# ScalarE's order in a fused layer: the second norm's deviations of tiles 2 and 3 ahead of two passes over tile 0

## The chip, the cores and the metric

The kernel runs on one core of a Trainium2 chip. The time is device microseconds of one execution. A core has five engines with an instruction queue each, worked off in order: TensorE (PE, with its weight loads PEld), VectorE (DVE), ScalarE (ACT), GpSimd (POOL) and SyncE (SP), which here only issues DMAs. An instruction that waits for a semaphore holds up everything behind it on its own engine.

## What is computed

One layer over a sequence of 2048 rows of 512 numbers, in bfloat16. A vector c, through SiLU and w_mod, gives six modulation rows. Then two branches, each with a residual:

```python
h = _layernorm(x) * (1 + ca) + sa
x = x + ga * A(h)          # dilated local attention, 32 heads of 16, window 8, dilation 2
h = _layernorm(x) * (1 + cb) + sb
x = x + gb * B(h)          # B norms h once more, then an MLP over the rows (2048 -> 1792 -> 2048)
```

So every row is normed three times: before the attention (norm 1), after it (norm 2, then scaled and shifted), and at the start of the MLP (norm 3). The MLP mixes rows, so it needs all tiles of rows for each of its 14 blocks of hidden units; the kernel adds up the products of the tiles as they become ready.

## The kernel before

The rows are 16 tiles of 128. The attention runs over five chunks of 2, 4, 4, 4 and 2 tiles (0 to 4); tiles 2 to 5 are chunk 1. Several chunks are under way at once. The kernel's helper functions do not emit instructions: they register named steps with their dependencies, and a text, ORDER, names all steps in the order in which they are emitted. An engine thus gets its steps in the order in which they stand in ORDER. A letter behind a colon picks the engine where a step has a choice (a is ScalarE, d VectorE, p POOL, s SyncE; q is a form of the matmul with four groups of columns). PSUM banks and the large work buffers are given out along ORDER too: a step that needs one takes the free one that was freed first in ORDER.

Steps that the change and the prediction speak of:

- `x1_t`, `ln2q_t`: ScalarE copies the residual sum of tile t out of PSUM, with its row sum, and then squares the deviations, with their sum. Both sums lie in `sums`.
- `rstd2_g`: the inverse deviations of norm 2 for a group of tiles that starts at g, two ScalarE instructions, `lv` = Ln(scaled sum + eps) and `rs` = Exp(-lv/2). Groups of chunk 1 are tiles 2, 3 and tiles 4, 5. `nb2_g` on VectorE makes the offset from the mean and `rs`; `n2_t` applies both; `aff_g` scales and shifts a group (two pairs of VectorE operations in all for tiles 2 to 5).
- `ln3s_t`, `ln3v_t`, `rstd3_g`, `nb3_g`, `h3_t`: the same for norm 3, statistics, their last step on VectorE, inverse deviations, offsets, normed tile. For tiles 0 and 1 the statistics are two ScalarE passes (a mean, then squares of what is left) into `mv`. For tiles 3 and 5 they are two ScalarE passes too, with a small VectorE operation (`ln3v3`, `ln3v5`) behind them; for 2 and 4 VectorE's batch statistics and an aggregate (`ln3v2`, `ln3v4`). `h3_0` and `h3_1` run on POOL, `h3_2` and `h3_3` on VectorE, `h3_4` and `h3_5` on ScalarE.
- `ev4_tj`: ScalarE copies queries (t = 0), keys (1) or values (2) of chunk 4 out of PSUM.
- `qk`, `red`, `max`, `sub`, `exp`, `esum`, `rcp`, `smB`, `a2`, `pv`, `pvacc`, `oev`, `wo`: the attention of a chunk. VectorE multiplies queries and keys (`qk`), TensorE sums (`red`), VectorE takes the maximum (`max`), TensorE subtracts it (`sub`), ScalarE takes the exponent (`exp`), TensorE sums it (`esum`), ScalarE inverts the sum (`rcp`, its result `rb`), VectorE scales (`smB`, in `lsb`), DMAs of SyncE rearrange (`a2`), VectorE multiplies with the values (`pv`), TensorE sums (`pvacc`), ScalarE copies out (`oev`), TensorE projects (`wo`).
- `mlp1_...`: the MLP's first matmuls, over a few tiles `h3` at a time.

The code behind `rstd`:

```python
nc.scalar.activation(lv[:, sl, 0], mv[:, sl, 1] if var is None else var, ACT.Ln, scale=vscale, bias=epscol[:, 0:1])
nc.scalar.activation(rs[:, sl, 0], lv[:, sl, 0], ACT.Exp, scale=-0.5)
```

In ORDER, ScalarE has around the place `ln2q2`, `ev4_20`, `ln3s0`, `ev4_12`, `rstd2_2`, `ev4_22`, `oev2_0`, `rstd2_4`, `n2_2`, `exp3`, `oev2_3`, `n2_5`, `rcp3`, `n2_4`, `oev2_2`, `rstd3_0`, `oev2_1`, `ev4_02`, `ln3s3`, `ev4_00`, `rstd3_2`. VectorE has `qk3_3`, `pv2_0`, `nb2_2`, `max3`, `pv2_2`, `nb2_4`, `pv2_1`, `smB3`, `aff2`, `aff4`, `nb3_0`, `ln3s2`, `ln3v3`, `ln3v2`, `ln3s4`, `ln3v4`, `h3_3`, `h3_2`, `pv3_1`. All instructions carry the line of the wrapper that emits them, L143, so the profile's rows are told apart by their operands and their time.

Of the kernel before, what the change touches and what calls it, by code (L numbers as in the profile page):

```python
# [213 lines left out]
fill:1:q vd2_0 oev1_0:a oev1_1:a pvacc1_3 ev3_11:a qk3_1 qkv3_23:q oev1_3:a a2_2_2:s ln3s1 qkv3_03:q wo4:q a2_2_1:s  # L214
qk3_2 a2_2_0:s ev3_03:a ev3_23:a x1_4:a ln2q4 wo2:q x1_2:a a2_2_3:s red3_0 wo3:q x1_3:a ln2q3 qkv3_21:q ev3_21:a wo5:q
red3_1 pv2_3 x1_5:a vd2_2 qk3_3 qkv4_20:q red3_2 qkv4_22:q red3_3 qkv4_12:q fill:18:q ln2q5 ld_w1_0_512 ln2q2 pv2_0
pvacc2_0 vd3_0 ev4_20:a ln3s0 ev4_12:a rstd2_2 ev4_22:a qkv4_02:q oev2_0:a rstd2_4 nb2_2 n2_2:a max3 sub3:q exp3
pvacc2_3 oev2_3:a qkv4_10:q pv2_2 vd3_2 esum3:q nb2_4 pv2_1 vd3_1 n2_3:p ld_w1_0_0 n2_5:a rcp3 smB3 pvacc2_2 fill:14:q
a2_3_0:s a2_3_1:s a2_3_3:s n2_4:a qkv4_00:q oev2_2:a rstd3_0 aff2 pvacc2_1 oev2_1:a wo6:q wo9:q wo7:q aff4 nb3_0
ln3s2:d ev4_02:a ln3s3:a ln3v3 h3_1:p wo8:q a2_3_2:s ev4_00:a ln3v2 ld_w2_0 ln3s4:d rstd3_2 x1_9:a ln3s5:a h3_0:p  # L220
# [857 lines left out]
```

## Time and profile before

| | us |
|---|---|
| three runs | 199.3, 199.72, 200.41 (median 199.72) |
| the profiled execution | 199.64 |
| its span, first to last instruction | 197.9 |
| mean granted TensorE clock | 0.999 |
| PE, DVE, ACT, POOL busy | 187.8, 157.5, 127.8, 18.5 |

The span is 1.74 us shorter than the execution's own time. A row of the timeline gives start, length, engine, operation, output and inputs, shapes and a count, and in brackets the time that the engine stood idle before it, with what ended the wait. Starts are from the first instruction. Instructions on one engine overlap a little: the next one starts some hundredths of a microsecond before the one ahead has written its last result.

### The profile page before, as it was taken

What the parts mean: (1) busy time and instruction counts of PE and PEld (TensorE: products, weight loads), DVE (VectorE), ACT (ScalarE), POOL (GpSimd) and SP (SyncE); (2) the same over time, 40 slices, a digit from 0 to 9 for tenths busy, and PEclk for the clock granted to TensorE, in tenths of its full rate; (3) what the DMA queues carried; (4) which work ended last, traced back from release to release, by engine and by line L of the source; (5) the groups of instructions that cost most, each with busy time, mean ns of one, the idle gap of its engine ahead of it and who ended that gap; (6) DMA issues with size and microseconds to landing.
All of it is one profiled execution on the core that took longest, in us unless ns stands there. A gap on an engine that the chain in (4) does not pass through costs nothing.

```text
span 197.9 us, 5606 instructions
## 1 busy us (share of the span) xinstructions
PE 187.8 (95%) x2348; PEld 101.9 (51%) x2358; DVE 157.5 (80%) x222; ACT 127.8 (65%) x305; POOL 18.5 (9%) x45
## 2 busy tenths in 40 slices
PE   2999999999999988999999999999999999999993
PEld 0586655655456676544544454444444444444453
DVE  2789999999999998999999999986564254726554
ACT  3898997998999999999999799833760000000000
POOL 4164002000100001030001100500000000000000
PEclk9999999999999999999999999999999999999999
DMA  5999985728678756379299367588999201111611
GB/s 171 325 358 321 219 227 164 156 57 260 230 223 285 236 191 215 105 159 298 40 332 227 76 209 143 156 241 233 329 224 325 74 0 53 39 44 53 172 53 53
DMA packets 53893, 36.02 MB, mean 182 GB/s; under 512 B 24428, under 2 KB 50668, under 8 KB 53868
## 3 DMA queue, kind: packets, MB, share of 16 engines
q1 hardware_dynamic: 52228, 35.21, 63.0%
q10 hardware_dynamic: 1640, 0.46, 1.0%
q8 instruction: 18, 0.29, 0.6%
q14 instruction: 7, 0.06, 0.1%
HBM read 22.55 MB, written 2.10 MB: 125 GB/s over the span
## 4 chain that ended last, share of the span: by engine, by line
PE 64%; ACT 19%; DVE 5%; DMA 4%; SPq 3%; issue 3%; ACTq 0%; DVEq 0%
PE psS L143 63%; ACT junk L143 4%; DMA vD<-v_sb 3%; SPq L143 3%; ACT xx L143 2%; ACT v_sb L143 2%; ACT h L143 2%; DVE big L143 2%; PE psL L143 2%; ACT q_sb L143 2%; ACT k_f L143 2%; DVE h L143 1%; ACT o_sb L143 1%; DMA c_t<-in_c_dram 1%; ACT lsb L143 1%
## 5 line engine op out<-in xcount | busy, mean ns | idle before, releaser
L143 PEld LDWEIGHTS <-wst 128*128 128x128 bf16 (+1 forms) x584 | 35.6, 101 | 33.0 <-issue 2.8
L143 PE MATMUL psS<-h,wst 128*32 128x512 bf16 (+1 forms) x358 | 50.5, 379 | 0.6 <-issue 0.2
L143 DVE TENSOR_TENSOR big<-q_sb,k_f 128x4096 bf16<-128x4096 bf16 (+1 forms) x20 | 36.6, 1857 | 0.1
L143 DVE TENSOR_TENSOR big<-a2sb,vD 128x4096 bf16<-128x4096 bf16 (+1 forms) x20 | 36.5, 1858 | 0.0
L143 PE MATMUL psS<-hT,w_qkv 128*32 128x512 bf16 (+1 forms) x576 | 29.6, 344 | 0.3 <-ACT o_sb L143 0.3
L143 DVE SCALAR_TENSOR_TENSOR h<-psS,bcol,rows_bc 128x512 f32<-128x512 f32 (+2 forms) x17 | 12.1, 710 | 22.1 <-PE psS L143 20.6
L143 PEld LDWEIGHTS <-w_qkv 128*32 128x32 bf16 (+1 forms) x618 | 22.1, 107 | 14.1 <-issue 0.5
L143 PE MATMUL psS<-gT,big 128*128 128x512 bf16 x110 | 24.7, 379 | 0.1
L143 PEld LDWEIGHTS <-big 128*128 128x128 bf16 x144 | 12.1, 98 | 13.8 <-DMA big<-in_w_mod_dram 0.5
L143 PE MATMUL psS<-woq,o_sb 128*32 128x512 bf16 (+1 forms) x207 | 16.7, 379 | 0.5 <-ACT o_sb L143 0.5
L143 ACT ACTIVATE gT<-psS,bcol 128x512 bf16<-128x512 f32 x14 | 9.0, 686 | 8.3 <-DVE psS L143 8.2
L143 POOL TENSOR_SCALAR h<-xx,rs,nb 128x512 bf16<-128x512 bf16 x9 | 7.0, 785 | 72.7 <-DVE nb L143 33.9
L143 DVE TENSOR_TENSOR psS<-psS,gT 128x512 f32<-128x512 f32 x14 | 9.3, 695 | 5.0 <-PE psS L143 5.0
L143 PE MATMUL psS<-hT,wst 128*32 128x512 bf16 (+2 forms) x135 | 11.7, 355 | 0.1
L143 ACT ACTIVATE h<-xx,nb,rs 128x512 bf16<-128x512 bf16 x15 | 11.6, 812 | 0.0
L143 DVE TENSOR_TENSOR h<-h,xx 128x512 bf16<-128x512 f32 (+2 forms) x17 | 11.1, 653 | 0.6
L143 PEld LDWEIGHTS <-group 128*32 128x32 bf16 x288 | 7.8, 96 | 7.2 <-issue 2.7
L143 DVE BATCH_NORM_STATS2 st<-xx 128x6 f32<-128x512 bf16 x12 | 8.0, 682 | 4.3 <-DMA xx<-in_A_x_dram 4.2
L143 DVE TENSOR_TENSOR h<-h,rows_bc 128x1024 bf16<-128x1024 bf16 (+2 forms) x16 | 10.9, 689 | 0.4
L143 ACT ACTIVATE junk<-xx,sums 128x512 bf16<-128x512 bf16 x14 | 10.1, 722 | 1.6 <-DVE xx L143 1.4
L143 ACT ACTIVATE v_sb<-psS,qvb 128x512 bf16<-128x512 f32 (+1 forms) x20 | 11.0, 597 | 0.0
L143 PEld LDWEIGHTS <-ident 128*32 128x32 bf16 (+2 forms) x242 | 7.1, 99 | 7.4 <-issue 2.8
(107 smaller groups left out, 252.4 us busy)
## 6 DMA issues: line engine op xcount, KB each, us to landing
vD<-v_sb SPq DMA_DIRECT2D x12, 524.5 KB, 3.7
big<-in_B_w_dram SPq DMA_DIRECT2D x4, 896.0 KB
vD<-v_sb SPq DMA_DIRECT2D x8, 268.5 KB, 5.1
wst<-in_B_w_dram SPq DMA_DIRECT2D x3, 640.0 KB
out_dram<-h SPq DMA_DIRECT2D x15, 128.0 KB, 1.8
wst<-in_B_w_dram SPq DMA_DIRECT2D x2, 800.0 KB
xx<-in_A_x_dram SPq DMA_DIRECT2D x6, 256.0 KB, 8.0
gT<-in_w_mod_dram SPq DMA_DIRECT2D x4, 384.0 KB, 4.7
```

The costliest lines, as they stand in the source:

```text
L143: r = fn(*a, **k)
```

## The change

One name in ORDER moves. `rstd2_2` stood behind `ev4_12` and now stands behind `ev4_20`, so ScalarE emits its two instructions ahead of `ln3s0` (the third norm's two passes over tile 0) and `ev4_12`. Its inputs are the sums that `ln2q2` and `ln2q3` leave. All other steps keep their order on every engine, and the step takes and frees no buffer.

```diff
-pvacc2_0 vd3_0 ev4_20:a ln3s0 ev4_12:a rstd2_2 ev4_22:a qkv4_02:q oev2_0:a rstd2_4 nb2_2 n2_2:a max3 sub3:q exp3
+pvacc2_0 vd3_0 ev4_20:a rstd2_2 ln3s0 ev4_12:a ev4_22:a qkv4_02:q oev2_0:a rstd2_4 nb2_2 n2_2:a max3 sub3:q exp3
```

## The prediction

> **What bounds the kernel now.** I read the engine totals and the chain of waits first, then a table of stretches around the edited place, then the waits and the timelines there. The page:
>
> ```profile
> PE 187.8 (95%) x2348; PEld 101.9 (51%) x2358; DVE 157.5 (80%) x222; ACT 127.8 (65%) x305; POOL 18.5 (9%) x45
> ...
> PE 64%; ACT 19%; DVE 5%; DMA 4%; SPq 3%; issue 3%; ACTq 0%; DVEq 0%
> ```
>
> TensorE sets most of the span, but 19% of the chain is ScalarE. Where that lies, the stretches show (length; busy time of PE, weight loads, DVE, ACT, POOL; granted clock; DMA):
>
> ```profile
> 72.00:76.00 4.00, 3.33 (x99) 2.44 (x95) 3.12 (x4) 3.94 (x12) 0.00 (x0) 1.00 0.64 239
> 76.00:82.00 6.00, 5.39 (x172) 3.90 (x164) 6.00 (x5) 5.94 (x14) 0.77 (x1) 1.00 0.72 227
> 82.00:87.00 5.00, 4.51 (x88) 2.03 (x80) 4.90 (x13) 4.73 (x15) 1.71 (x3) 1.00 0.27 64
> 87.00:92.00 5.00, 4.88 (x92) 2.36 (x84) 5.00 (x7) 4.94 (x18) 0.00 (x0) 1.00 1.16 297
> ```
>
> From 72 to 92 us ScalarE is never free: 3.94 of 4 us, 5.94 of 6, 4.94 of 5. VectorE is equally full except in the first stretch, where 0.88 us are missing. The waits between 72 and 94 us name that hole and one more on ScalarE:
>
> ```profile
> DVE nb L143 <- ACT rs L143: 0.9, 1, 0.9
> ...
> ACT lv L143 <- DVE mv L143: 0.2, 1, 0.2
> ```
>
> These are the two joints of the forecast. The chain of waits shows where ScalarE hands the end over to TensorE (start, length, what):
>
> ```profile
> 92.30 1.42 ACT h L143 x2
> 93.72 0.04 issue
> 93.76 3.09 PE psS L143 x52
> ```
>
> So h3_4 and h3_5 (the two "ACT h") release matmuls at 93.76, and from there on the chain is TensorE's own work almost to the last instruction. A gain on ScalarE at 92 us reaches the end; a gain on VectorE alone does not.
>
> **The change part by part.** The step rstd2_2 is two ScalarE instructions (Ln into lv, Exp into rs), with no DMA, nothing on SP or POOL, no buffer taken or freed. ScalarE in the order of time:
>
> ```profile
> 72.63 0.82 ACT L143 ACTIVATE v_sb<-psS,qvb 128x256 bf16<-128x256 f32 x2
> ...
> 74.81 0.57 ACT L143 ACTIVATE k_f<-psS 128x512 bf16<-128x512 f32 x1
> 75.29 0.28 ACT L143 ACTIVATE lv<-sums,epscol 128x2 f32<-128x2 f32 x1
> 75.60 0.20 ACT L143 ACTIVATE rs<-lv 128x2 f32<-128x2 f32 x1
> 75.71 0.82 ACT L143 ACTIVATE v_sb<-psS,qvb 128x256 bf16<-128x256 f32 x2
> ...
> 80.45 0.31 ACT L143 ACTIVATE rb<-ls 128x128 bf16<-128x128 f32 x1
> ```
>
> *Moved earlier.* The pair occupies 75.71 - 75.29 = 0.42 us. It goes to where the first v_sb row ends, 72.63 + 0.82 - 0.09 = 73.36 (an instruction here starts about 0.09 before the one ahead has drained: 74.81 + 0.57 = 75.38 against 75.29). rs is then there at about 73.87 instead of 75.80. Nothing is added or removed, so ScalarE's work from 72.63 to 75.71 is the same length, and v_sb at 75.71 stays.
>
> *Moved later.* The third norm's two passes over tile 0 (ln3s0) and the key copy ev4_12 come 0.42 later. The first is needed by rstd3_0, behind the rb row above, five microseconds on. The copy frees a PSUM bank at 75.38, now 75.80; by the kernel's bank rule its next taker is the sum of exponents, and the keys themselves are read only by chunk 4's products, behind all of chunk 3's in VectorE's queue:
>
> ```profile
> 79.11 0.63 PE L143 MATMUL psS<-lsb,ident 128*32 128x128 bf16 x32
> ```
>
> That leaves 3.3 us of cover; both cost nothing. Without the cover the price would be the 0.42.
>
> *VectorE.* Its timeline, with idle time and releaser in brackets:
>
> ```profile
> 72.67 2.28 DVE L143 TENSOR_TENSOR big<-a2sb,vD 128x4096 bf16<-128x4096 bf16 x1
> 75.84 0.16 DVE L143 SCALAR_TENSOR_TENSOR nb<-sums,rs 128x2 f32<-128x2 f32 x1 [0.88 <-ACT rs L143]
> 75.92 1.22 DVE L143 TENSOR_REDUCE m<-psL 128x128 bf16<-128x1024 f32 x1
> 77.05 2.28 DVE L143 TENSOR_TENSOR big<-a2sb,vD 128x4096 bf16<-128x4096 bf16 x1
> ...
> 79.32 2.29 DVE L143 TENSOR_TENSOR big<-a2sb,vD 128x4096 bf16<-128x4096 bf16 x1
> 81.52 0.68 DVE L143 TENSOR_TENSOR lsb<-lsb,rb 128x1024 bf16<-128x1024 bf16 x1
> ...
> 83.45 1.41 DVE L143 TENSOR_TENSOR h<-h,rows_bc 128x1024 bf16<-128x1024 bf16 x2
> ...
> 84.78 0.15 DVE L143 SCALAR_TENSOR_TENSOR nb<-mv,rs 128x2 f32<-128x2 f32 x1
> 84.85 0.69 DVE L143 BATCH_NORM_STATS2 st<-h 128x6 f32<-128x512 bf16 x1
> 85.45 0.43 DVE L143 SCALAR_TENSOR_TENSOR mv<-mv,st 128x1 f32<-128x1 f32 x1
> 85.81 0.17 DVE L143 BATCH_NORM_AGGREGATE mv<-st 128x2 f32<-128x6 f32 x1
> ```
>
> nb2_2 (75.84) stood 0.88 us with everything behind it: max3, pv2_2, nb2_4, pv2_1, smB3. With rs there at 73.87 it starts at 74.96, or 74.88 with the usual overlap; the queue gains 0.88 to 0.96. What is late next is rb: smB3 needs it, and ScalarE ends it at 80.45 + 0.31 = 80.76, unmoved. pv2_1 would be through at 81.52 - 0.88 = 80.64 at the latest, so smB3 starts at 80.79 (0.03 after rb, as 75.84 followed 75.60 + 0.20 by 0.04). VectorE keeps 0.73 of 0.88. On TensorE, sub3 starts earlier, but its sum of exponents at 79.11 waits for exp3 on ScalarE, ahead of which no instruction waits for VectorE: TensorE's hole only moves.
>
> *What ScalarE gets back.* It is full, so only waits of its own can shrink. There are three, each read as start minus (end of the one before, minus 0.09):
>
> ```profile
> 82.16 0.20 ACT L143 ACTIVATE rs<-lv 128x2 f32<-128x2 f32 x1
> 82.33 0.60 ACT L143 ACTIVATE o_sb<-psS 128x512 bf16<-128x512 f32 x1
> 82.82 0.83 ACT L143 ACTIVATE q_sb<-psS,qvb 128x256 bf16<-128x256 f32 x2
> 83.63 0.63 ACT L143 ACTIVATE junk<-h 128x512 bf16<-128x512 bf16 x1
> ...
> 84.92 0.19 ACT L143 ACTIVATION_READ_ACCUMULATOR junk<-h 128x1 f32 x1
> 85.02 0.82 ACT L143 ACTIVATE q_sb<-psS,qvb 128x256 bf16<-128x256 f32 x2
> 86.01 0.29 ACT L143 ACTIVATE lv<-mv,epscol 128x2 f32<-128x2 f32 x1 [0.17 <-DVE mv L143]
> ```
>
> 1. o_sb at 82.33 (oev2_1) against 82.36 - 0.09 = 82.27: 0.06. It waits for matmuls fed by pv2_1. TensorE may keep part of it, so 0 to 0.06; I take 0.04.
> 2. junk at 83.63 (ln3s3) against 83.65 - 0.09 = 83.56: 0.07. It waits for aff2, done as the second pair of "h" operations starts at 83.45; with VectorE 0.73 ahead it waits no more.
> 3. lv at 86.01 (rstd3_2) against 85.84 - 0.09 = 85.75: 0.26, if its mv is ready in time.
>
> Is it? ln3v3 (the 0.43 us row at 85.45) needs ln3s3's read, 84.92 + 0.19 = 85.11, less 0.11 from items 1 and 2: 85.00, so it starts at 85.03, VectorE being there since 85.45 - 0.73 = 84.72. At most 0.43 us long, it and the 0.17 us aggregate end by 85.03 + (85.81 - 85.45) + 0.17 = 85.56, plus 0.03: 85.59. ScalarE reaches its lv at 85.75 - 0.11 = 85.64. Just in time, so item 3 counts whole.
>
> The sum is 0.04 + 0.07 + 0.26 = **0.37 us** (bounds: 0 if item 3 and the others are taken away by the rivals below, 0.88 if the whole hole came through). ScalarE has no other wait up to 93.72, so h3_5 ends 0.37 earlier. TensorE stands waiting there:
>
> ```profile
> 93.76 1.20 PEld L143 LDWEIGHTS <-wst 128*32 128x32 bf16 x27 [0.45 <-issue]
> ```
>
> 0.45 is more than 0.37, so TensorE can take all of it; the stalls before it follow ScalarE's copies too and shrink alike. Past 94 us loads are issued when TensorE releases their buffers, so they move along.
>
> One resource can spoil item 3. POOL forms h3_1 and h3_0 right after VectorE's nb3_0, beside ln3v3:
>
> ```profile
> 85.11 1.53 POOL L143 TENSOR_SCALAR h<-h,rs,nb 128x512 bf16<-128x512 bf16 x2 [8.18 <-DVE nb L143]
> ...
> 89.51 0.21 DVE L143 SCALAR_TENSOR_TENSOR mv<-mv,st 128x1 f32<-128x1 f32 x1
> ```
>
> The same operation takes 0.21 with POOL idle and 0.43 beside POOL, ending at 85.88, when half of POOL's 1.53 is over (85.11 + 0.77). The Trainium skill, "SBUF — State Buffer", section "SBUF: two separate sides", says that VectorE with two SBUF inputs and GpSimd take a shared port pair as an exclusive lock, the loser blocked for a whole instruction; by that rule the two rows agree, and an arrival behind the second POOL instruction would wait for that one's end. After the change POOL starts at 84.78 - 0.73 + (85.11 - 84.78) = 84.38 and passes from h3_1 to h3_0 at 85.15; ln3v3 arrives at 85.03, only 0.12 before. I take the near side, with the rival below as the far one.
>
> **The numbers.** The profiled execution took 199.64 us (span 197.9 and 1.74 around it); 199.64 - 0.37 = 199.27. That execution is 0.08 under the median of 199.72, so I put the figure for a median at 199.3.
>
> **The rivals.**
> - *The hole comes through whole*: 199.64 - 0.88 = 198.76. For it: VectorE is as full as ScalarE from 76 us on, and every later instruction of it was queued behind the hole. Against: rb at 80.76 and ln3s3 are ScalarE's, and no wait of ScalarE before 82.33 depends on VectorE. Chance 0.15.
> - *Nothing arrives*: the bracket at 93.76 reads "issue", not "ACT h". If another thing, such as a weight buffer, released TensorE there, its stream keeps its place: 199.64, or 199.60 with item 1. Against: h ends 93.72, 0.04 before. Chance 0.14.
> - *Slower, through POOL*: if ln3v3 is ready after 85.15, it is held until h3_0 ends, 84.38 + 1.53 = 85.91. Ending there, as the row of 85.45 ended with its POOL instruction, it puts lv at 85.91 - 0.07 + 0.17 + 0.03 = 86.04: 0.03 later than now, 199.67. Starting only there, it adds its 0.21: lv at 86.25, 0.24 later, 199.88. It decides from a slip of 0.12 us in my chain of starts on. For it: the slip is the size of three unknown overlaps. Against: those rows give the near side. Chance 0.14.
>
> **How the numbers follow.** The forecast has 0.47, the rivals 0.15, 0.14 and 0.14, and 0.10 is left for what I don't see, half on each side. The likeliest case alone spans 199.15 to 199.5. To hold 8 in 10, the range takes in the rivals and the scatter of the shown runs (199.3 to 200.41, which moves a median by some tenths): 198.6 to 200.0. A measurement of this kernel tells about 0.5%, 1 us, from no change. Faster by more than that (below 198.72): half of the first rival 0.08, a tenth of the forecast through scatter 0.05, half of the unseen 0.05: 0.18. Slower (above 200.72): a third of the POOL rival through scatter 0.05, 0.04 from the forecast and the second rival, 0.05 unseen: 0.14. Within: 0.68.
>
> **What would show it.** Right: the 0.88 bracket before nb2_2 gone; max3 near 74.95; a new short wait of VectorE for rb, smB3 near 80.8; lv of rstd3_2 near 85.64 without a bracket; the chain's passage from ACT h to PE near 93.4; a span near 197.5. The first rival would show smB3 at 80.64 or before, with rb earlier than 80.76. The POOL rival would show mv<-mv,st ending with the second POOL instruction near 85.9. The second would show TensorE still starting at 93.76 with h long done. I am wrong altogether if ScalarE's starts between 75.71 and 82 us shift by more than 0.1, or if the granted clock in these stretches leaves 1.00.

## The result, and the profile after

| | us | ratio to before (95% interval) |
|---|---|---|
| before, 22 runs beside it | median 199.55 (199.21 to 201.13) | |
| after, 22 runs | median 199.04 (198.82 to 200.0) | 0.9969 (0.9956 to 0.9982) |
| after, measured once more: 11 runs, before 199.67 | median 199.33 (199.01 to 199.65) | 0.9981 (0.9971 to 0.9992) |

The kernel is faster by 0.2 to 0.3%: the first ratio says 0.62 us (the two medians alone differ by 0.51), the second 0.38. The trace says 0.42 from the edited place to the end, which both intervals hold. The profiled execution took 199.34 us with a span of 197.6.

First the waits of the changed kernel between 72 and 94 us (who waited for whom, us in total, times, longest):

```profile
PE psS L143 <- ACT lsb L143: 0.8, 1, 0.8
...
DVE mv L143 <- ACT junk L143: 0.2, 1, 0.2
DVE lsb L143 <- ACT rb L143: 0.2, 1, 0.2
```

VectorE's 0.9 for rs is gone, and so is ScalarE's 0.2 for mv. In their place VectorE waits twice for ScalarE, 0.2 each. TensorE's hole of 0.6 ahead of sub3 is now one of 0.8 ahead of the sum of exponents. VectorE's timeline (start, length, operation, idle time before it):

```profile
72.80 2.29 DVE L143 TENSOR_TENSOR big<-a2sb,vD 128x4096 bf16<-128x4096 bf16 x1
75.00 0.15 DVE L143 SCALAR_TENSOR_TENSOR nb<-sums,rs 128x2 f32<-128x2 f32 x1
75.07 1.22 DVE L143 TENSOR_REDUCE m<-psL 128x128 bf16<-128x1024 f32 x1
...
80.91 0.69 DVE L143 TENSOR_TENSOR lsb<-lsb,rb 128x1024 bf16<-128x1024 bf16 x1 [0.15 <-ACT rb L143]
...
85.13 0.22 DVE L143 SCALAR_TENSOR_TENSOR mv<-mv,st 128x1 f32<-128x1 f32 x1 [0.20 <-ACT junk L143]
```

The last row is the small step `ln3v3`. POOL's pair `h3_1` and `h3_0` runs beside it:

```profile
84.50 1.53 POOL L143 TENSOR_SCALAR h<-h,rs,nb 128x512 bf16<-128x512 bf16 x2 [8.41 <-DVE nb L143]
```

ScalarE has no bracket left where it had one:

```profile
72.75 0.82 ACT L143 ACTIVATE v_sb<-psS,qvb 128x256 bf16<-128x256 f32 x2
73.46 0.29 ACT L143 ACTIVATE lv<-sums,epscol 128x2 f32<-128x2 f32 x1
73.78 0.20 ACT L143 ACTIVATE rs<-lv 128x2 f32<-128x2 f32 x1
...
82.40 0.60 ACT L143 ACTIVATE o_sb<-psS 128x512 bf16<-128x512 f32 x1
82.90 0.83 ACT L143 ACTIVATE q_sb<-psS,qvb 128x256 bf16<-128x256 f32 x2
83.61 0.64 ACT L143 ACTIVATE junk<-h 128x512 bf16<-128x512 bf16 x1
...
85.00 0.82 ACT L143 ACTIVATE q_sb<-psS,qvb 128x256 bf16<-128x256 f32 x2
85.72 0.29 ACT L143 ACTIVATE lv<-mv,epscol 128x2 f32<-128x2 f32 x1
```

The starts of two executions can't be set against each other as they stand. This one came to the edited place 0.12 us later than the one before (v_sb at 72.75, then 72.63), for reasons ahead of any change. So from here on times count from that v_sb row, ScalarE's last common step ahead of the edit. The release of TensorE by h3_5 reads in the weight loads:

```profile
93.47 1.63 PEld L143 LDWEIGHTS <-wst 128*32 128x32 bf16 x34 [0.45 <-issue]
```

That is 93.47 - 72.75 = 20.72 after and 93.76 - 72.63 = 21.13 before: 0.41. The wait in front of it is 0.45 as before, because the weight loads ahead of the wait moved up as well, from 92.36 - 72.63 = 19.73 to 92.06 - 72.75 = 19.31. Their rows, before and after:

```profile
92.36 0.96 PEld L143 LDWEIGHTS <-wst 128*32 128x32 bf16 x20 [0.20 <-issue]
```

```profile
92.06 0.96 PEld L143 LDWEIGHTS <-wst 128*32 128x32 bf16 x20 [0.20 <-issue]
```

The last group in the chain of waits is VectorE's last operation, 2.7 us ahead of the end of the span in both profiles:

```profile
194.59 0.29 DVE h L143
```

194.59 - 72.75 = 121.84, against 194.89 - 72.63 = 122.26 before: 0.42. So what TensorE gained at 93 us it kept for the following hundred.

### The profile page after: what moved, and what is told of

Read it like the earlier page. It is cut to its first block, busy times and chain, and to the rows that moved or that the text cites. A ratio compares the mean times of both kernels' runs of the same rounds, so it can differ in the third digit from the quotient of the medians.

```text
span 197.6 us, 5606 instructions
## 1 busy us (share of the span) xinstructions
PE 187.6 (95%) x2348; PEld 102.1 (52%) x2358; DVE 157.8 (80%) x222; ACT 127.6 (65%) x305; POOL 18.9 (10%) x45
## 4 chain that ended last, share of the span: by engine, by line
PE 61%; ACT 20%; DVE 7%; DMA 4%; issue 4%; SPq 3%; ACTq 0%; DVEq 0%
PE psS L143 59%; ACT junk L143 4%; DMA vD<-v_sb 3%; SPq L143 3%; ACT xx L143 2%; ACT v_sb L143 2%; DVE big L143 2%; ACT h L143 2%; ACT q_sb L143 2%; ACT o_sb L143 2%; PE psL L143 2%; DVE st L143 2%; ACT k_f L143 1%; DMA c_t<-in_c_dram 1%; ACT lsb L143 1%
```

## The experiments

The expectations measure from pv2_0 on VectorE. That row starts 0.04 us after v_sb before and between 0.04 and 0.20 (e3) after it in the runs, so the table counts from v_sb; there 21.09 and 20.68 of the expectations are 21.13 and 20.72. "Release" is the weight load that stood waiting for h3_5, "end" the last group of the chain. Each ratio is to the kernel before, measured beside the run.

| run | release | end | median us | ratio (interval) |
|---|---|---|---|---|
| before | 21.13 | 122.26 | | |
| after | 20.72 | 121.84 | 199.04 | 0.9969 (0.9956 to 0.9982) |
| e1_nb_behind_max | 20.71 | 121.83 | 199.26 | 0.9976 (0.9949 to 1.0003) |
| e2_half_way | 20.72 | 121.84 | 199.16 | 0.9982 (0.9961 to 1.0003) |
| e3_late_small_step | 21.16 | 122.29 | 199.70 | 0.9999 (0.9983 to 1.0015) |
| e4_rcp_first | 21.03 | 122.15 | one run, 199.57 | |
| e5_h5_vector | no wait there | 122.01 | 199.60 | 1.0002 (0.9982 to 1.0022) |
| e6_extra_scalar | 21.21 | 122.33 | 199.72 | 0.9992 (0.9975 to 1.0010) |
| e7_fill_holes | 20.70 | 121.78 | 199.25 | 0.9986 (0.9967 to 1.0006) |
| e8_after_again | 20.71 | 121.83 | 199.33 | 0.9981 (0.9971 to 0.9992) |

The runs scatter by more than these effects, and all intervals but those of the changed kernel hold 1; the verdicts rest on the traces, whose release and end repeat to 0.01 us in the changed kernel (after and e8). The kernel before has one trace. The ratios agree with the traces within their intervals.

**e1: the wait on VectorE, removed in another way**

```diff
-... rstd2_4 nb2_2 n2_2:a max3 sub3:q exp3
+... rstd2_4 max3 nb2_2 n2_2:a sub3:q exp3
```

> The kernel before with one VectorE step moved: the offsets of tiles 2 and 3 (nb2_2) stand behind the maximum (max3) instead of ahead of it; ScalarE's order is that of before. Measure: from the start of pv2_0 on VectorE (72.67 before, 72.80 after) to the start of the matmuls that h3_5 releases (93.76 before, 93.48 after): 21.09 before, 20.68 after. Theory (the wait on VectorE was the whole matter, and ScalarE's own three waits carry the gain): VectorE loses the same 0.88, so 20.68 and about 0.41 us less time than before, although ScalarE's order is the old one. Rival (ScalarE's new order itself brings it): 21.09, no change in time. Beside it: POOL's n2_3 now asks for its start while pv2_2 runs; if the two exclude each other, it starts only some 2 us later, at no cost for the end.

The end is 0.43 earlier than before, with ScalarE's order of before. So removing the wait on VectorE is enough for the whole gain, and what ScalarE does first adds nothing that the trace shows. VectorE and POOL in this run:

```profile
75.16 1.22 DVE L143 TENSOR_REDUCE m<-psL 128x128 bf16<-128x1024 f32 x1
76.29 0.15 DVE L143 SCALAR_TENSOR_TENSOR nb<-sums,rs 128x2 f32<-128x2 f32 x1
76.36 2.29 DVE L143 TENSOR_TENSOR big<-a2sb,vD 128x4096 bf16<-128x4096 bf16 x1
78.56 0.15 DVE L143 SCALAR_TENSOR_TENSOR nb<-sums,rs 128x2 f32<-128x2 f32 x1
78.64 2.28 DVE L143 TENSOR_TENSOR big<-a2sb,vD 128x4096 bf16<-128x4096 bf16 x1
81.07 0.94 DVE L143 TENSOR_TENSOR lsb<-lsb,rb 128x1024 bf16<-128x1024 bf16 x1 [0.15 <-ACT rb L143]
```

```profile
76.61 4.87 POOL L143 TENSOR_SCALAR h<-xx,rs,nb 128x512 bf16<-128x512 bf16 x1 [23.37 <-PE psS L143]
```

The maximum starts with no wait ahead of it. POOL's n2_3, 0.77 us long elsewhere, takes 4.87: it came 0.25 into pv2_2 and ended at 81.48, after pv2_1, and smB3 beside it took 0.94 instead of 0.69. The expectation had put it some 2 us late; it was over 4. VectorE lost 0.25 by it, and the release and the end did not move.

**e2: half of the way up**

```diff
-pvacc2_0 vd3_0 ev4_20:a ln3s0 ev4_12:a rstd2_2 ev4_22:a ...
+pvacc2_0 vd3_0 ev4_20:a ln3s0 rstd2_2 ev4_12:a ev4_22:a ...
```

> The kernel before with rstd2_2 only half way up: behind the two passes over tile 0, ahead of the key copy. rs is there 0.48 us earlier than before instead of 1.9, so VectorE's wait shrinks from 0.88 to about 0.40. Theory (what counts are the three waits of ScalarE, and they need only some 0.4 of VectorE's time): still 0.36 to 0.41 us of gain, measure at most 20.73. Rival (the gain goes with the time VectorE gets back): 0.48 of 0.88, so about 0.22 us, measure near 20.87.

VectorE still waits for nearly half of the time:

```profile
75.79 0.16 DVE L143 SCALAR_TENSOR_TENSOR nb<-sums,rs 128x2 f32<-128x2 f32 x1 [0.41 <-ACT rs L143]
```

The whole gain is there all the same: 20.72 and 121.84. The gain does not go with VectorE's time; ScalarE's three waits need no more than the 0.47 of 0.88 that VectorE has back here.

**e3: the small step behind POOL's second instruction**

```diff
-ln3s2:d ev4_02:a ln3s3:a ln3v3 h3_1:p wo8:q a2_3_2:s ev4_00:a ln3v2 ld_w2_0 ln3s4:d rstd3_2 ...
+ln3s2:d ev4_02:a ln3s3:a ln3s4:d ln3v3 h3_1:p wo8:q a2_3_2:s ev4_00:a ln3v2 ld_w2_0 rstd3_2 ...
```

> The changed kernel with VectorE's batch statistics of tile 4 (ln3s4) ahead of the small step ln3v3, so that ln3v3 comes some 0.3 us later, when POOL has passed on to h3_0. Theory with exclusion between POOL and this step: ln3v3 lasts until POOL's second instruction is over (about 0.55 us instead of 0.22), lv of rstd3_2 starts at or after the 86.01 of before, the gain is gone (measure 21.05 to 21.15, time as before). Without exclusion: ln3v3 lasts 0.21 and lv is late by the 0.3 of the order alone, less ScalarE's margin: measure 20.80, two thirds of the gain kept.

VectorE, POOL and ScalarE in this run:

```profile
84.15 1.28 DVE L143 BATCH_NORM_STATS2 st<-h 128x6 f32<-128x512 bf16 x2
85.35 0.58 DVE L143 SCALAR_TENSOR_TENSOR mv<-mv,st 128x1 f32<-128x1 f32 x1
```

```profile
84.41 1.52 POOL L143 TENSOR_SCALAR h<-h,rs,nb 128x512 bf16<-128x512 bf16 x2 [8.27 <-DVE nb L143]
```

```profile
86.05 0.30 ACT L143 ACTIVATE lv<-mv,epscol 128x2 f32<-128x2 f32 x1 [0.33 <-DVE mv L143]
```

The step takes 0.58 instead of 0.22 and ends at 85.93, with POOL's pair (84.41 + 1.52 = 85.93). ScalarE waits 0.33 and the end is 122.29, 0.03 past before. This is the slower rival of the prediction made to happen, on its near side: that put lv 0.03 later than before; here lv starts 86.05 - 72.65 = 13.40 after v_sb, 0.02 later than before, and the release came 0.03 later.

**e4: rb earlier**

```diff
-... n2_5:a rcp3 smB3 ...
+... rcp3 n2_5:a smB3 ...
```

> The changed kernel with ScalarE's inverse of the sum of exponents (rcp3) ahead of the normed tile 5 (n2_5), so that rb is there some 0.5 us earlier and VectorE's new wait of 0.15 us ahead of smB3 goes. Theory (VectorE's time beyond what ScalarE's three waits need is worth nothing): smB3 0.15 earlier, the wait ahead of ln3v3 0.15 longer, measure 20.68 as after. Rival (VectorE's queue sets the end): measure 20.53.

A miss, and a useful one: the release fits neither the theory nor the rival. VectorE's wait ahead of smB3 went, but ScalarE now came to the sum of exponents before TensorE had it:

```profile
79.83 0.28 ACT L143 ACTIVATE ls<-psS 128x128 f32<-128x128 f32 x1 [0.24 <-PE psS L143]
```

```profile
80.63 0.69 DVE L143 TENSOR_TENSOR lsb<-lsb,rb 128x1024 bf16<-128x1024 bf16 x1
...
85.37 0.37 DVE L143 SCALAR_TENSOR_TENSOR mv<-mv,st 128x1 f32<-128x1 f32 x1 [0.73 <-ACT junk L143]
```

smB3 starts 80.63 - 72.67 = 7.96 after v_sb, in the changed kernel 80.91 - 72.75 = 8.16: VectorE is 0.20 ahead. The end is 0.31 later (122.15 against 121.84), about the 0.24 that ScalarE stood still and the 0.09 of overlap that a wait costs it. The small step was held here too (0.37), but ScalarE was late enough not to wait for it. VectorE earlier, end later: the rival that VectorE's queue sets the end is out.

**e5: what releases TensorE at 93 us**

```diff
-... h3_5:a ...
+... h3_5:d ...
```

> The changed kernel with the normed tile 5 (h3_5) on VectorE instead of ScalarE. Theory (TensorE's 0.45 us of waiting near 93.5 ends with h3_5): the wait goes, the matmuls that stood there start about 0.4 earlier (measure near 20.3), ScalarE has 0.7 us back; VectorE's queue is 0.33 later, so part or all of it is given back at the values' products (pvacc3_3), and the end is between 0.3 us better and 0.2 worse than the changed kernel. Rival (something else, a weight buffer, releases those matmuls): they start as in the changed kernel, 20.68.

The wait of 0.45 is gone, and only the 0.20 that the changed kernel has too is left earlier on; the weight loads run through, where the changed kernel stopped before 93.47, and the 80 matmuls around it take 4.58 us instead of 4.91. (Weight loads, then matmuls, of e5.)

```profile
92.15 1.41 PEld L143 LDWEIGHTS <-wst 128*32 128x32 bf16 x31 [0.20 <-issue]
```

```profile
96.68 0.62 PE L143 MATMUL psS<-h,wst 128*32 128x512 bf16 x8
97.85 0.61 PE L143 MATMUL psS<-big,group 128*32 128x512 bf16 x8 [0.55 <-DVE big L143]
```

So h3_5 was the releaser, although the bracket reads "issue". The gain is given back at the values' products: TensorE waits 0.55 there for VectorE, which carries the 0.41 us of h3_5 now. The end, 122.01, is 0.17 worse than the changed kernel.

**e6: half a microsecond more on ScalarE**

```diff
             nc.scalar.activation(lv[:, sl, 0], ...
             nc.scalar.activation(rs[:, sl, 0], lv[:, sl, 0], ACT.Exp, scale=-0.5)
+            if name == "3_0":
+                nc.scalar.activation(junk[:], xx[:, 5, :], ACT.Identity)
```

> The changed kernel with one more ScalarE instruction, a copy of tile 5 into the unused buffer, ahead of rstd3_0 (behind rb, so VectorE's part up to smB3 is untouched). It adds 0.5 to 0.6 us to ScalarE. Theory (ScalarE sets the release near 93.5): measure 21.2 to 21.3 and all of it in the time, 0.5 to 0.6 more than the changed kernel. Rival (VectorE or TensorE sets it, and ScalarE has slack): at most 0.2 later.

The copy stands behind the two instructions of rstd3_0, not ahead of them as the expectation has it, and so still behind rb. It occupies ScalarE for 0.52 (it starts at 82.97, the next instruction at 83.49). The release moves from 20.72 to 21.21 and the end from 121.84 to 122.33, both by 0.49. What is added to ScalarE here is, but for 0.03, added to the kernel in the trace; the medians, taken at different times, are no test as fine as this. The small step again ended with POOL's second instruction (it took 0.41), with ScalarE late enough to cover it.

**e7: the same kind of move at three later places, and e8: the changed kernel again**

```diff
-... qk4_2 n2_7:d qk4_3 ...
+... qk4_2 qk4_3 n2_7:d ...
...
-... smB4 a2_4_1:a a2_4_0:s mlp1_0_9_4 a2_4_2:s h3_9:d a2_4_3:a ...
+... h3_9:d smB4 a2_4_1:a a2_4_0:s mlp1_0_9_4 a2_4_2:s a2_4_3:a ...
...
-... pv4_2 nb2_10 ld_w1_1_0 pv4_1 ...
+... pv4_2 ld_w1_1_0 pv4_1 nb2_10 ...
```

> The changed kernel with the same kind of move at three later places of VectorE's queue: the normed tile 7 of the first norm pair (n2_7) behind qk4_3, the normed tile 9 (h3_9) ahead of smB4, where VectorE waits some 0.3 us for rcp4, and the offsets nb2_10 behind pv4_1, where it waits some 0.35 us for rstd2_10. Theory (TensorE from 93 to 102 us still stands about 0.25 us at red4_3 and wo11 for VectorE and ScalarE, and is its own bound after that): 0.1 to 0.25 us better than the changed kernel, if nothing takes the place of those waits by 120 us. Rival (TensorE's stalls there are those of its own form changes, or ScalarE's copies follow at once): no change against the changed kernel, within 0.05 us in the trace.

> The changed kernel once more, beside the run above. Its first profile shows 0.42 us less from the edited place to the end; the ratio of the first runs said 0.62, with 0.36 to 0.88 us as its bounds. If 0.42 is the whole effect, the ratio comes near 0.998; if something outside the traced chain helps as well, near 0.997.

e7 ends at 121.78, 0.06 better than the changed kernel in the trace, less than the 0.1 to 0.25 expected and just outside the rival's 0.05, and 0.9986 beside 0.9981 says that no difference is to be measured. TensorE has little to win there: in the changed kernel it is busy for 35.74 of the 36 us from 94 to 130. Nor were VectorE's waits removed: between 94 and 130 they come to 1.8 us in both runs, with new ones in the place of the old, so e7 does not show what they cost. Why TensorE keeps a part of its stall around wo11 when VectorE is early was not settled. e8 gives 121.83 in the trace and 0.9981 in time, 0.38 us. That fits with the 0.42 of the traces as the whole effect and a part of the 0.62 of the first ratio as scatter.

## Why the prediction was right

It forecast 199.3, by 0.37 us (its own sum, 199.27 and 0.08 for a median, gives 199.35); the median is 199.04, the second measurement 199.33, and the traces show 0.41 to 0.42. That the second median lies so near is in part luck, as medians of one kernel differ by 0.3.

- *The hole on VectorE*, 0.88: gone; nb2_2 and the maximum start at pv2_0's end. smB3 moved from 81.52 - 72.63 = 8.89 to 8.16, by 0.73 as worked out, with a wait for rb in front.
- *Costs of what came later*, nothing: e1 moves neither the passes over tile 0 nor the key copy, and ends alike.
- *Item 1* (oev2_1), 0.04 of 0 to 0.06: 9.70 became 9.65, 0.05. TensorE kept next to nothing.
- *Item 2* (ln3s3), 0.07: 11.00 became 10.86, 0.14 with item 1, so 0.09.
- *Item 3* (rstd3_2), 0.26: 13.38 became 12.97, 0.41 in all, so 0.27.
- *The small step in time*: ln3v3 was put at 85.03 and POOL at 84.38 on the clock of before. Less the 0.12 of this execution they came at 85.01 and 84.38. ln3v3 took 0.22 and not the 0.43 that the prediction allowed, although POOL's first instruction still had 0.14 to run (it starts at 84.50 and is half of the 1.53, so 85.27; the step starts at 85.13).
- *TensorE takes it all at 93 us*: 0.41 there and 0.42 at the end; e5 shows that h3_5 is the releaser. The 0.45 of waiting was not what paid for it: it stayed 0.45, as the weight loads ahead of it were already 0.42 earlier. What held is the other half of the sentence, that the stalls before it shrink alike. That these follow ScalarE's copies is not shown: the profile puts them down to "issue", and no run tries it.
- *Rivals.* That the whole hole comes through fell with the 0.42 itself, and with e2 and e4; that nothing arrives fell with e5 and e6. The POOL rival did not come about, but e3 shows that it was real and how near: a slip of the small step past POOL's hand-over from h3_1 to h3_0, 0.14 away, costs the whole gain.
- *One test was badly put.* "ScalarE's starts shift by more than 0.1" would have condemned a right forecast: they shifted by 0.12, all of it from ahead of the edit. It should have said "from a row ahead of the edit".

## What to carry to other kernels

A wait in a full queue is worth what the next full engine can use of it: follow the freed time forward to the first input that it doesn't control (here rb, unmoved, took 0.15 of the 0.88), then add up the waits of the engine that carries the chain (0.05 + 0.09 + 0.27; a little over half of the relief, 0.47, bought them in e2). Compare traces from the last common row ahead of the edit. A small result of another engine belongs, in an in-order queue, behind work that is ready (e1), unless that pushes a POOL instruction that something waits for under VectorE's long ones (n2_3 in e1, at no cost to the end there).

## What the runs showed of the hardware

POOL and some VectorE instructions exclude each other, and the hold can outlast one instruction. The small step with two operands in SBUF took 0.21 to 0.22 us alone. Where POOL made it longer (0.37 to 0.58: before, e1 to e4 and e6), it ended within 0.01 us of the end of a POOL instruction, as at 85.88 before and at 85.93 in e3. The same operation near 13 us met POOL in all ten traces: it took 0.35 to 0.52 and ended within 0.01 us of POOL's end each time. Where POOL's instruction had less left than the step's own 0.22 (0.14 in the changed kernel), the step was not longer.

In e1 POOL's 0.77 us of work took 4.87. It was through at neither change from one VectorE instruction to the next, pv2_2 to the small nb2_4 to pv2_1: it ended at 81.48, 0.56 after pv2_1. The batch statistics beside POOL, 84.85 to 85.54 before with POOL from 85.11, took 0.69; without POOL they take 0.66 to 0.70.

The Trainium skill, "SBUF — State Buffer", section "SBUF: two separate sides", calls the shared port pair an exclusive lock whose loser waits for the whole instruction. The runs agree, and show that a loser can lose more than once (4.87 us here).
